# Values in 32 KB rows, one ring of four buffers, and value products moved behind the second half of the scores

## The chip, the cores and the metric

The kernel runs on one core of a Trainium2 chip. The metric is the device time of one execution in microseconds (us); the core has TensorE (PE, its weight loads shown as PEld), VectorE (DVE), ScalarE (ACT), GpSimd (POOL) and SyncE (SP), which work through their own instruction queues in order and wait for one another by semaphores. The loads from HBM are issued by SP, apart from one small one by ACT, and carried by 16 DMA engines.

## The reference

One token (B = S = 1, D = 512) goes through a decode step of grouped-query attention over a cache of 16384 tokens, with 32 query heads of 128 elements, 8 key/value heads and 4 query heads to each of them, and then through a small MLP. All inputs are bf16.

```python
def _A_ref(x, k_cache, v_cache, wq, wo):
    q = (x @ wq).reshape(B, Sq, Hq, Dh).transpose(0, 2, 1, 3)
    k = jnp.repeat(k_cache, rep, axis=1)          # k_cache: 1 x 8 x 16384 x 128
    v = jnp.repeat(v_cache, rep, axis=1)
    scores = jnp.einsum("bhqd,bhkd->bhqk", q, k) * (Dh ** -0.5)
    p = _softmax(scores, axis=-1)
    o = jnp.einsum("bhqk,bhkd->bhqd", p, v)
    return o.transpose(0, 2, 1, 3).reshape(B, Sq, Hq * Dh) @ wo

def _B_ref(x, w1, w2, w3, w4):
    ...
    x1 = x + hs          # hs is 0 for a single token: its shifted parts are all padding
    h2 = _gelu(_layernorm(x1) @ w3) @ w4
    return x1 + h2

h = x + _A_ref(_layernorm(x), ...)
return h + _B_ref(_layernorm(h), ...)
```

The keys and the values of one head are 4 MB each, so the two caches are 64 MB. `wq` and `wo` are 4 MB each, `w3` and `w4` 1.75 MB each.

## The kernel before, in words

**Loading.** `load` (L215) puts every big transfer on SP's queue, in program order. SP holds each issue until the buffer it writes is free, and whatever stands behind it on SP waits too. Keys of a head come as one transfer of 128 rows of 32 KB (`load_k`, L218) into one of two buffers `kb` (`KRING`, L124). Values come as two transfers of 128 rows of 16 KB, one for each half A of the tokens (`load_v`, L230), into three buffers `vb` of half a head (`VRING`, L125); the last head's values go to `kb[0]`. `wq` and later `wo` use the buffer `wqo`, `w3` and `w4` the buffer `kb[1]`. The order on SP is wq, k0, k1, and then in iteration g of the main loop both halves of v(g) and k(g+2), and in iteration 7 the last values and the weights.

**The main loop** (L472) runs over g = 0 to 8. In iteration g it does the scores and the softmax of head g and the value products of head g-1:

- `transpose_keys` (L385): eight DVE block transposes of 1024 words each, tiles t = 0 to 7, from `kb` to `kt`. The one buffer `kt` holds the head being worked on.
- `scores(g, half)` (L395): 16 matmuls of 512 columns for each half of the scores, into the PSUM tile `s_ps`. Four matmuls at a time use the four column groups (`ct`) of the array; the first one on column group ct of a half needs tile t = 4*half + ct, so the last 13 of a half start when its last transpose is done.
- `max_a`, `max_b`, `max_c` (L406, L410, L418): a maximum over all tokens, by a DVE reduction of each half, two small matmuls, a second reduction, and a matmul that spreads it over the partitions; then two ACT exponentials (L425) of 512 columns write the weights `p_sb`. A POOL copy repeats the first columns at its end.
- `weights(g)` (L433): 16 PE transposes of windows of 128 columns, 64 apart, into the two-bank PSUM tile `T_ps` (eight to a bank), and five DVE copies (L441) from it into `pt`.
- `denominator` (L445), and `gather(g-1)` (L462): one DVE copy of `O_ps` to `o_sb` and four fp32 matmuls (each recorded as two) that lay the head's output into `A_ps`.
- `values(g-1, A, qs)` (L450): 16 matmuls of 512 columns for each half A of the tokens. They are placed by hand on PE: the 16 of half 0 between the two halves of the scores, 8 of half 1 before `max_b` and 8 before `max_c`.

In iteration 0, when there are no values yet, three of the next head's key transposes are done early. Iteration 8 has only the values and the gather of head 7.

**The end.** The output is normalised (L520 to L527), multiplied by `wo` (128 matmuls, L533, in four pieces as they land), and goes through the layer norm (`row_sums` L255, `variance` L268, `seeds` L277, `inverse_root` L293), `w3` (L546), Gelu (L558), `w4` (L567) and the store (L573).

`Program.op` (L35) derives the waits: an operation waits for the last writer of what it reads, for the writers and readers of what it writes, and for the last operation of every other engine on a PSUM bank that it touches.

Of the kernel before, what the change touches and what calls it, by code (L numbers as in the profile page):

```python
# [7 lines left out]
BF16 = mybir.dt.bfloat16  # L8
# [102 lines left out]
D = 512  # L111
HQ = 32
# [11 lines left out]
KRING = 2  # L124
VRING = 3  # L125
VT = 64 * DH
KPARTS = 6
# [4 lines left out]
def bass_sequential_preLN__gqa_block_cached__mixer_s_mlp__decode_kernel(  # L132
# [13 lines left out]
    with ExitStack() as ctx:  # L146
# [3 lines left out]

# [33 lines left out]
        p_sb = sb("p_sb", [128, 1024 + 64], BF16)  # L184
        pt = [sb(f"pt{i}", [128, 4, 2, 16, REP], BF16) for i in range(2)]
# [14 lines left out]
        wqo = sb("wqo", [128, NCH * HQ * DH], BF16)  # L200
        kb = [sb(f"kb{i}", [128, 128 * DH], BF16) for i in range(KRING)]
        kt = sb("kt", [128, 128 * DH], BF16)
        vb = [sb(f"vb{i}", [128, VT], BF16) for i in range(VRING)]
        w3_sb = kb[1][:, 0:NCH * FM].rearrange("p (k f) -> p k f", k=NCH)
        w4_sb = kb[1][:, NCH * FM:2 * NCH * FM].rearrange("p (m c) -> p m c", m=NHC)
# [12 lines left out]
        def load_k(g):  # L218
            i = g % KRING
            load(f"k{i}", kb[i][:, :], A_k_cache[0, g].rearrange("(p t) d -> p (t d)", p=128), ("k", i, 0),  # L220
                 also=[("k", i, n) for n in range(1, KPARTS)])

        def value_tile(g, A):

            if g == HKV - 1:
                return kb[0][:, A * VT:(A + 1) * VT], ("k", 0, A)
            i = (2 * g + A) % VRING
            return vb[i][:, :], ("v", i)

        def load_v(g, A):  # L230
            src = A_v_cache[0, g, A * 8192:(A + 1) * 8192, :].rearrange("(p t) d -> p (t d)", p=128)
            dst, key = value_tile(g, A)
            load("v" + "_".join(map(str, key[1:])), dst, src, key)
# [59 lines left out]
        def inverse_root(i, n, by):  # L293

            s, t = st[i], sti[i]
            S, T = ("st", i), ("sti", i)
            v, y = s[:, 4 + n:5 + n], t[:, n:n + 1].bitcast(FP32)
            z = s[:, 8 + n:9 + n]
            vh = s[:, 10 + n:11 + n]
            by(lambda e: e.tensor_scalar(vh, v, -0.5, None, ALU.mult), r=[(S, 4 + n)], w=[(S, 10 + n)])  # L300
            for k in range(3):
                dst, key = (s[:, 6 + n:7 + n], (S, 6 + n)) if k == 2 else (y, (T, n))
                by(lambda e: e.tensor_scalar(z, y, y, vh, ALU.mult, ALU.mult),
                   r=[(T, n), (S, 10 + n)], w=[(S, 8 + n)])
                by(lambda e, dst=dst: e.tensor_scalar(dst, z, 1.5, y, ALU.add, ALU.mult),
                   r=[(S, 8 + n), (T, n)], w=[key])
# [3 lines left out]
        load("wq", wqo[:, :], A_wq.rearrange("(p k) c -> p (k c)", k=NCH), ("wo", 0),  # L310
             also=[("wo", n) for n in range(1, len(WO))])
        load_k(0)
        load_k(1)
# [52 lines left out]
        for h in range(HQ):  # L366
            for k in range(NCH):
                pe(lambda e, h=h, k=k: e.matmul(n_ps[:, h:h + 1],  # L368
                                                wqo[:, k * HQ * DH + h * DH:k * HQ * DH + (h + 1) * DH],
                                                xn[:, k:k + 1], start=(k == 0), stop=(k == NCH - 1)),  # L370
                   r=["xn"] + [("wo", n) for n in range(len(WO))], w=["n"], bank=["mn"])
# [13 lines left out]
        def transpose_keys(g, ts):  # L385
            i = g % KRING
            for t in ts:
                view = lambda x, t=t: x[:, :].bitcast(I32).rearrange("p (x l w) -> p x (l w)", x=2, l=64)[
                    :, :, t * 512:(t + 1) * 512]
                dve(lambda e, i=i, view=view: e.transpose(view(kt), view(kb[i])),  # L390
                    r=[("k", i, n) for n in range(KPARTS)], w=[("kt", t)])

        ktv = kt[:, :].rearrange("p (x l b s e) -> p b e l x s", x=2, l=64, b=2, s=32, e=2)

        def scores(g, half):  # L395
            for n in range(4):
                for ct in range(4):
                    c8 = 4 * half + ct
                    pe(lambda e, g=g, half=half, n=n, ct=ct, c8=c8: e.matmul(  # L399
                        s_ps[32 * ct:32 * ct + 32, half, :],  # L400
                        qb[:, n, g, :, :, :].rearrange("p a u h -> p (a u h)"),
                        ktv[:, n // 2, n % 2, 8 * c8:8 * c8 + 8, :, :],
                        start=(n == 0), stop=(n == 3)),
                       r=["qb", ("kt", c8)], w=[("s", half)], bank=[("s", half)])
# [13 lines left out]
        def max_c(g):  # L418
# [5 lines left out]
            for half in range(2):  # L424
                act(lambda e, half=half, g=g: e.activation(  # L425
                    p_sb[:, half * 512:half * 512 + 512].rearrange("p (l s x) -> p l x s", l=8, x=2),
                    s_ps[:, half, :].rearrange("p (l x s) -> p l x s", l=8, x=2),
                    ACTF.Exp, bias=bias[:, 0:1], scale=float(SCALE), accum_out=acc[g % 2][:, half:half + 1]),
                    r=[("s", half), "bias"], w=[("p", half), ("acc", g % 2)], bank=[("s", half)])
                if half == 0:  # L430
                    P.op("POOL", lambda e: e.tensor_copy(p_sb[:, 1024:1088], p_sb[:, 0:64]), r=[("p", 0)], w=[("p", 2)])  # L431

        def weights(g):  # L433
            for w in range(16):
                pe(lambda e, w=w: e.transpose(T_ps[:, w, :], p_sb[:, w * 64:w * 64 + 128], ident[:, :]),  # L435
                   r=[("p", w // 8), ("p", (w + 1) // 8), "ident"], w=[("T", w // 8)], bank=[("T", w // 8)])
            to = pt[g % 2][:, :, :, :, :].rearrange("p c A l h -> p l (c A) h")
            of = T_ps[:, :, :].rearrange("p w (k o u h) -> p w k o u h", o=2, u=2, h=REP)
            for half, lo, w0, w1, l0 in ((0, 0, 0, 8, 0), (0, 64, 0, 8, 1), (1, 0, 8, 16, 8), (1, 64, 8, 15, 9),
                                         (1, 64, 15, 16, 0)):  # L440
                dve(lambda e, lo=lo, w0=w0, w1=w1, l0=l0: e.tensor_copy(  # L441
                    to[lo:lo + 64, l0:l0 + w1 - w0, :, :], of[lo:lo + 64, w0:w1, :, lo // 64, 0, :]),
                    r=[("T", half)], w=[("pt", g % 2)], bank=[("T", half)])
# [6 lines left out]
        def values(g, A, qs):  # L450
            tile, key = value_tile(g, A)
            for q in qs:
                for ct in range(4):
                    n = 32 * (q // 2) + 8 * ct + 4 * (q % 2)
                    pe(lambda e, q=q, ct=ct, n=n: e.matmul(  # L455
                        O_ps[g % 2][32 * ct:32 * ct + 16, :],
                        pt[g % 2][:, ct, A, 4 * q:4 * q + 4, :].rearrange("p l h -> p (l h)"),
                        tile[:, n * DH:(n + 4) * DH],
                        start=(A == 0 and q == 0), stop=(A == 1 and q == 3)),
                       r=[key, ("pt", g % 2)], w=[("O", g % 2)], bank=[("O", g % 2)])  # L460
# [11 lines left out]
        for g in range(HKV + 1):  # L472
# [6 lines left out]
            if g:  # L479
                values(g - 1, 0, range(4))  # L480
            if g < HKV:
                scores(g, 1)
                max_a(1)
            if g == 0:
                transpose_keys(1, range(0, 1))
            if g:
                values(g - 1, 1, range(2))
            if g < HKV:
                max_b()
            if g:  # L490
                values(g - 1, 1, range(2, 4))
            if g < HKV:
                max_c(g)
            if g == 0:
                transpose_keys(1, range(1, 3))
# [5 lines left out]
            if g < HKV:  # L501
                for A in range(2):
                    load_v(g, A)
                if g + 2 < HKV:
                    load_k(g + 2)
            if g == HKV - 1:
                for n, (lo, hi) in enumerate(WO):
                    load(f"wo{n}", wqo[:, lo * D:hi * D], A_wo.rearrange("(p r) c -> p (r c)", p=128)[:, lo * D:hi * D],
                         ("wo", n))
                w3_in = B_w3.rearrange("(p k) f -> p k f", p=128)  # L510
                for n, (lo, hi) in enumerate(W3):
                    load(f"w3{n}", w3_sb[:, lo:hi, :], w3_in[:, lo:hi, :], ("k", 1, n))
                w4_in = B_w4.rearrange("(p m) c -> p m c", p=128)
                for n, (lo, hi) in enumerate(W4):
                    load(f"w4{n}", w4_sb[:, lo:hi, :], w4_in[:, lo:hi, :], ("k", 1, 2 + n))
# [15 lines left out]
        for r_ in range(32):  # L531
            for q in range(4):
                pe(lambda e, r_=r_, q=q: e.matmul(O_ps[0][32 * q:32 * q + 32, 0:128], copies(o_b[:, r_:r_ + 1], 32),  # L533
                                                  wqo[:, r_ * D + q * 128:r_ * D + (q + 1) * 128],
                                                  start=False, stop=(r_ == 31), skip_group_check=True),
                   r=["o_b", ("wo", piece(WO, r_))], w=[("O", 0)], bank=[("O", 0)])
# [7 lines left out]
        for k in range(NCH):  # L544
            for q in range(4):
                pe(lambda e, k=k, q=q: e.matmul(s_ps[32 * q:32 * q + 32, 0, 0:FQ], hc[:, k, :],  # L546
                                                w3_sb[:, k, q * FQ:(q + 1) * FQ], start=(k == 0), stop=(k == NCH - 1)),
                   r=["hc", ("k", 1, piece(W3, k))], w=[("s", 0)], bank=[("s", 0)])
# [16 lines left out]
        for m in range(NHC):  # L565
            for o in range(4):
# [3 lines left out]
                   r=[("hcol", 2 * m // NHC), ("k", 1, 2 + piece(W4, m))], w=["n"], bank=["mn"])  # L570
# [36 lines left out]
```

## Time and profile before

| | |
|---|---|
| time, median of 3 runs (lowest to highest) | 193.95 us (193.8 to 193.97) |
| time of the profiled execution | 194.09 us |
| its span, first to last instruction | 192.3 us |
| busy: PE / DVE / ACT / POOL | 112.8 / 120.1 / 16.9 / 6.6 us |
| key transposes, L390 (64) | 74.0 us, 1212 ns each |
| score matmuls, L399 (256) | 556 ns each, four at a time |
| value matmuls, L455 (224 and 32) | 529 and 474 ns each, four at a time |
| copies of weights, L441, 64x256 (24) | 286 ns each |
| copies of weights, L441, 64x224 (8) / 64x32 (8) | 278 / 172 ns each |
| exponentials, L425 (16) | 824 ns each |
| mean granted TensorE clock | 0.761 of full speed |

The span is the time in which the core's instructions ran; the rest of the execution's time, 1.8 us, lies around it. Matmul durations contain the way through the array, so a stream of them is read from their starts: four value matmuls follow four others 0.42 us later at half clock and 0.21 us later at full clock. The clock that the throttle grants is 0.5 or 1.0 in this trace and changes every few microseconds. The trace also has a record of each DMA packet: a row of 16 KB is one packet of 613 ns (median of the 16 KB packets), a row of 32 KB one packet of 1214 ns (median of those).

### The profile page before, as it was taken

The numbers are of one execution on the slowest core, as the hardware profiler recorded it, in microseconds if no ns is written. First come the engines' busy times: TensorE is split into PE (matmuls) and PEld (weight loads), VectorE is DVE, ScalarE is ACT, GpSimd is POOL, SyncE is SP. The second block draws the span as 40 slices with busy tenths as digits, with TensorE's granted clock in tenths as the row PEclk, the third lists the DMA queues.
The fourth block names the chain that finished last, engine by engine and source line by source line (L and its number), as shares of the span: only waits on it lengthen the run. The fifth ranks groups of instructions, "written<-read, shape, count | busy, mean of one in ns | idle before, by whom it ended". The sixth has DMA issues, their size and how long they took to land.

```text
span 192.3 us, 2626 instructions
## 1 busy us (share of the span) xinstructions
PE 112.8 (59%) x1106; PEld 55.9 (29%) x1106; DVE 120.1 (62%) x225; ACT 16.9 (9%) x38; POOL 6.6 (3%) x26
## 2 busy tenths in 40 slices
PE   1025045658837766774686558645785676595443
PEld 1025001242234235223422432233223422454311
DVE  4844099499349929964795369546953796303170
ACT  3000000030030030003000300030003000600010
POOL 2000000000000000000000000000000000000060
PEclk9999999999985695588559655975558559669555
DMA  6999999999999999999999999999999999999991
GB/s 232 436 429 429 433 436 426 436 441 433 406 426 464 429 392 426 477 433 392 423 447 419 429 416 433 443 433 416 447 445 412 402 429 423 426 418 421 417 376 48
DMA packets 5066, 79.32 MB, mean 413 GB/s; under 512 B 576, under 2 KB 576, under 8 KB 1344
## 3 DMA queue, kind: packets, MB, share of 16 engines
q1 hardware_dynamic: 5048, 79.17, 96.9%
q8 instruction: 8, 0.13, 0.3%
q14 instruction: 2, 0.02, 0.0%
q10 hardware_dynamic: 8, 0.00, 0.0%
HBM read 79.17 MB, written 0.00 MB: 412 GB/s over the span
## 4 chain that ended last, share of the span: by engine, by line
DMA 40%; DVE 14%; SPq 5%; issue 2%; PE 1%
DMA kb<-in_A_k_cache_dram 30%; DVE kt L390 13%; DMA kb<-in_B_w_dram 10%; SPq L216 5%; DVE mx L407 1%; PE T_ps L435 0%; DVE pt L441 0%; PE mn_ps L567 0%; DVE fin L571 0%; PE A_ps L446 0%; SPq L102 0%; DVE o_sb L464 0%
## 5 line engine op out<-in xcount | busy, mean ns | idle before, releaser
L390 DVE STREAM_TRANSPOSE kt<-kb 128x1024 int32<-128x1024 int32 x64 | 74.0, 1212 | 11.2 <-DMA kb<-in_A_k_cache_dram 11.1
L399 PE MATMUL s_ps<-kt,qb 128*32 128x512 bf16 x256 | 47.5, 556 | 32.3 <-DVE kt L390 32.3
L455 PE MATMUL O_ps<-vb,pt 128*16 128x512 bf16 x224 | 28.9, 529 | 0.0
L399 PEld LDWEIGHTS s_ps<-kt,qb 128*32 128x32 bf16 x256 | 10.6, 113 | 61.9 <-DVE kt L390 54.1
L425 ACT ACTIVATE p_sb<-s_ps,bias 128x512 bf16<-128x512 f32 x16 | 12.8, 824 | 150.1 <-PE mn_ps L419 114.1
L467 PE MATMUL A_ps<-o_sb,zo 128*128 128x128 f32 x64 | 15.7, 422 | 10.3 <-DVE o_sb L464 10.3
L441 DVE COPY pt<-T_ps 64x256 bf16<-64x256 bf16 (+2 forms) x40 | 9.8, 261 | 15.6 <-PE T_ps L435 15.2
L407 DVE TENSOR_REDUCE mx<-s_ps 128x1 f32<-128x512 f32 x16 | 10.8, 677 | 11.9 <-PE s_ps L399 9.9
L435 PE MATMUL T_ps<-ident,p_sb 128*128 128x128 bf16 x128 | 11.8, 250 | 10.9 <-ACT p_sb L425 10.9
L467 PEld LDWEIGHTS A_ps<-o_sb,zo 128*128 128x128 f32 x64 | 13.4, 310 | 11.4 <-DVE o_sb L464 11.4
L435 PEld LDWEIGHTS T_ps<-ident,p_sb 128*128 128x128 bf16 x128 | 8.9, 112 | 12.9 <-ACT p_sb L425 12.7
L455 PEld LDWEIGHTS O_ps<-vb,pt 128*16 128x16 bf16 x224 | 9.4, 114 | 9.8 <-issue 8.5
L368 PE MATMUL mn_ps<-xn,wqo 128*128 128x1 bf16 x128 | 3.6, 165 | 9.1 <-DMA wqo<-in_A_wq_dram 9.1
L412 PE MATMUL mn_ps<-ident_f,mx 128*1 128x128 f32 x32 | 7.3, 323 | 2.5 <-DVE mx L407 2.5
L464 DVE COPY o_sb<-O_ps 128x512 f32<-128x512 f32 x8 | 5.5, 691 | 4.9 <-PE O_ps L455 4.6
L431 POOL COPY p_sb<-p_sb 128x64 bf16<-128x64 bf16 x8 | 1.9, 236 | 160.7 <-ACT p_sb L425 160.7
L368 PEld LDWEIGHTS mn_ps<-xn,wqo 128*128 128x128 bf16 x128 | 3.5, 104 | 9.2 <-issue 9.2
L415 DVE TENSOR_REDUCE nm<-mn_ps 1x4 f32<-1x256 f32 x8 | 3.2, 406 | 3.7 <-PE mn_ps L412 3.7
L533 PE MATMUL O_ps<-wqo,o_b 128*32 128x128 bf16 x128 | 3.0, 253 | 3.0 <-DMA wqo<-in_A_wo_dram 1.7
L412 PEld LDWEIGHTS mn_ps<-ident_f,mx 128*1 128x1 f32 x32 | 2.3, 90 | 7.7 <-DVE mx L407 5.4
L419 PEld LDWEIGHTS mn_ps<-nm,nscale 1*128 1x128 f32 x16 | 2.5, 198 | 5.5 <-DVE nm L415 5.5
L258 DVE TENSOR_SCALAR_CACHE_REDUCE hr<-O_ps 128x128 f32<-128x128 f32 x2 | 0.6, 292 | 5.5 <-PE O_ps L533 4.8
(79 smaller groups left out, 55.9 us busy)
## 6 DMA issues: line engine op xcount, KB each, us to landing
kb<-in_A_k_cache_dram SPq DMA_DIRECT2D x8, 4096.0 KB, 26.7
vb<-in_A_v_cache_dram SPq DMA_DIRECT2D x14, 2048.0 KB, 24.4
wqo<-in_A_wq_dram SPq DMA_DIRECT2D x1, 4096.0 KB, 12.4
kb<-in_A_v_cache_dram SPq DMA_DIRECT2D x2, 2048.0 KB, 26.6
wqo<-in_A_wo_dram SPq DMA_DIRECT2D x2, 1280.0 KB, 32.8
kb<-in_B_w_dram SPq DMA_DIRECT2D x1, 1344.0 KB, 22.9
wqo<-in_A_wo_dram SPq DMA_DIRECT2D x1, 1024.0 KB, 36.2
kb<-in_B_w_dram SPq DMA_DIRECT2D x1, 640.0 KB, 24.8
```

Of the source, the lines that this page charges most:

```text
L216: P.op(by, lambda e: e.dma_start(dst, src), w=[key, *also], dma=name)
L368: pe(lambda e, h=h, k=k: e.matmul(n_ps[:, h:h + 1], wqo[:, k * HQ * DH + h * DH:k * HQ * DH + (h + 1) * DH], xn[:, k:k + 1], start=(k == 0 ...
L390: dve(lambda e, i=i, view=view: e.transpose(view(kt), view(kb[i])), r=[("k", i, n) for n in range(KPARTS)], w=[("kt", t)])
L399: pe(lambda e, g=g, half=half, n=n, ct=ct, c8=c8: e.matmul(s_ps[32 * ct:32 * ct + 32, half, :], qb[:, n, g, :, :, :].rearrange("p a u h -> ...
L407: dve(lambda e: e.tensor_reduce(mx[:, half:half + 1], s_ps[:, half, :], AX.X, ALU.max), r=[("s", half)], w=[("mx", half)], bank=[("s", half)])
L412: pe(lambda e, half=half: e.matmul(m_ps[0:1, half * 128:half * 128 + 128], mx[:, half:half + 1], ident_f[:, :], start=True, stop=True), r= ...
L425: act(lambda e, half=half, g=g: e.activation(p_sb[:, half * 512:half * 512 + 512].rearrange("p (l s x) -> p l x s", l=8, x=2), s_ps[:, hal ...
L435: pe(lambda e, w=w: e.transpose(T_ps[:, w, :], p_sb[:, w * 64:w * 64 + 128], ident[:, :]), r=[("p", w // 8), ("p", (w + 1) // 8), "ident"] ...
L441: dve(lambda e, lo=lo, w0=w0, w1=w1, l0=l0: e.tensor_copy(to[lo:lo + 64, l0:l0 + w1 - w0, :, :], of[lo:lo + 64, w0:w1, :, lo // 64, 0, :]) ...
L455: pe(lambda e, q=q, ct=ct, n=n: e.matmul(O_ps[g % 2][32 * ct:32 * ct + 16, :], pt[g % 2][:, ct, A, 4 * q:4 * q + 4, :].rearrange("p l h -> ...
L464: dve(lambda e, g=g: e.tensor_copy(o_sb[g % 2][:, :], O_ps[g % 2][:, :]), r=[("O", g % 2)], w=[("osb", g % 2)], bank=[("O", g % 2)])
L467: pe(lambda e, g=g, j=j: e.matmul(A_ps[:, 0:128], zo[:, j, 112 - 16 * g:240 - 16 * g], o_sb[g % 2][:, j * 128:(j + 1) * 128], start=False, ...
```

## The change

All five big buffers and the value ring are replaced by four buffers `rb` of 32 KB a partition. One list, `ORDER`, gives the sequence of the loads: wq, k0, k1, then v0, k2, v1, k3, and so on to v7, wo, and the MLP weights; the n-th one uses buffer n mod 4. A head's values are one transfer of 128 rows of 32 KB, laid out like the keys.

With that, a partition's tokens lie otherwise in the score tile: the columns of a half are ordered (x, l, s) where they were permuted to (l, s, x) by the exponential's output. The exponential now writes plainly. The windows of the PE transposes stand 32 columns apart, and there are 32 of them in four fills of eight (f = 0 to 3); fills 0 and 2 use bank 0 of `T_ps` and are copied by DVE, fills 1 and 3 use bank 1 and are copied by ACT. A copy takes 32 partitions with 128 elements each. In fill 3 three of the four copies are split where the tokens wrap, so that it has seven. That makes 8 DVE copies and 11 ACT copies for each head. The POOL copy is of 96 columns.

All value products stand behind both halves of the scores: 8 before `max_b`, 8 before `max_c`, 16 after `max_c` and ahead of the PE transposes. In `inverse_root` the DVE form of one operation becomes `scalar_tensor_tensor`.

```diff
-KRING = 2
-VRING = 3
-VT = 64 * DH
-KPARTS = 6
+RING = 4
+ORDER = [("wq", 0), ("k", 0), ("k", 1)]
+ORDER += [x for g in range(HKV) for x in (("v", g), ("k", g + 2)) if x[1] < HKV] + [("wo", 0), ("ffn", 0)]
+SLOT = {x: n % RING for n, x in enumerate(ORDER)}
+QB, PB, FB = SLOT["wq", 0], SLOT["wo", 0], SLOT["ffn", 0]
+RPARTS = 6
...
-        p_sb = sb("p_sb", [128, 1024 + 64], BF16)
-        pt = [sb(f"pt{i}", [128, 4, 2, 16, REP], BF16) for i in range(2)]
+        p_sb = sb("p_sb", [128, 1024 + 96], BF16)
+        pt = [sb(f"pt{i}", [128, 4, 32, REP], BF16) for i in range(2)]
...
-        wqo = sb("wqo", [128, NCH * HQ * DH], BF16)
-        kb = [sb(f"kb{i}", [128, 128 * DH], BF16) for i in range(KRING)]
+        rb = [sb(f"rb{i}", [128, 128 * DH], BF16) for i in range(RING)]
         kt = sb("kt", [128, 128 * DH], BF16)
-        vb = [sb(f"vb{i}", [128, VT], BF16) for i in range(VRING)]
...
+        def load_whole(i, src):
+            load(f"r{i}", rb[i][:, :], src, ("r", i, 0), also=[("r", i, n) for n in range(1, RPARTS)])
+
+        def load_tokens(kind, g):
+            src = A_k_cache if kind == "k" else A_v_cache
+            load_whole(SLOT[kind, g], src[0, g].rearrange("(p t) d -> p (t d)", p=128))
...
-        ktv = kt[:, :].rearrange("p (x l b s e) -> p b e l x s", x=2, l=64, b=2, s=32, e=2)
+        ktv = kt[:, :].rearrange("p (x l b s e) -> p b e x l s", x=2, l=64, b=2, s=32, e=2)
...
-                        ktv[:, n // 2, n % 2, 8 * c8:8 * c8 + 8, :, :],
+                        ktv[:, n // 2, n % 2, :, 8 * c8:8 * c8 + 8, :],
...
-                    p_sb[:, half * 512:half * 512 + 512].rearrange("p (l s x) -> p l x s", l=8, x=2),
-                    s_ps[:, half, :].rearrange("p (l x s) -> p l x s", l=8, x=2),
+                    p_sb[:, half * 512:half * 512 + 512], s_ps[:, half, :],
...
-            for w in range(16):
-                pe(lambda e, w=w: e.transpose(T_ps[:, w, :], p_sb[:, w * 64:w * 64 + 128], ident[:, :]),
-                   r=[("p", w // 8), ("p", (w + 1) // 8), "ident"], w=[("T", w // 8)], bank=[("T", w // 8)])
...
+            of = T_ps[:, :, :].rearrange("p w (c a u h) -> p c w a u h", c=4, a=4, u=2)
+            for f in range(4):
+                b = f % 2
+                for w in range(8 * f, 8 * f + 8):
+                    pe(lambda e, w=w: e.transpose(T_ps[:, w % 16, :], p_sb[:, w * 32:w * 32 + 128], ident[:, :]),
+                       r=[("p", w // 16), ("p", (w + 3) // 16), "ident"], w=[("T", b)], bank=[("T", b)])
+                for a in range(4):
+                    n = 8 * f + a
+                    for lo, hi in ((n, min(n + 8, 32)), (32, n + 8)):
+                        if lo >= hi:
+                            continue
+                        args = (pt[g % 2][32 * a:32 * a + 32, :, lo % 32:lo % 32 + hi - lo, :],
+                                of[32 * a:32 * a + 32, :, 8 * b + lo - n:8 * b + hi - n, a, 0, :])
+                        if b == 0:
+                            dve(lambda e, args=args: e.tensor_copy(*args),
+                                r=[("T", b)], w=[("pt", g % 2, 0)], bank=[("T", b)])
+                        else:
+                            act(lambda e, args=args: e.copy(*args),
+                                r=[("T", b)], w=[("pt", g % 2, 1)], bank=[("T", b)])
...
-            if g:
-                values(g - 1, 0, range(4))
-            if g < HKV:
                 scores(g, 1)
                 max_a(1)
...
             if g:
-                values(g - 1, 1, range(2))
+                values(g - 1, range(2))
             if g < HKV:
                 max_b()
             if g:
-                values(g - 1, 1, range(2, 4))
+                values(g - 1, range(2, 4))
             if g < HKV:
                 max_c(g)
+            if g:
+                values(g - 1, range(4, 8))
...
             if g < HKV:
-                for A in range(2):
-                    load_v(g, A)
+                load_tokens("v", g)
                 if g + 2 < HKV:
-                    load_k(g + 2)
+                    load_tokens("k", g + 2)
```

## The prediction

> **What bounds the kernel now.** I read the page first, then the chain of waits, then the timeline of iterations 1, 3 and 5, then the granted clock by stretches.
>
> ```profile
> span 192.3 us, 2626 instructions
> ...
> DMA  6999999999999999999999999999999999999991
> ...
> q1 hardware_dynamic: 5048, 79.17, 96.9%
> ```
>
> The DMA engines never pause between the first load and the last, so bytes set the end. The chain of waits agrees, its long pieces being transfers. But compute is close behind:
>
> ```profile
> 57.34 1.23 DVE L390 STREAM_TRANSPOSE kt<-kb 128x1024 int32<-128x1024 int32 x1
> ...
> 74.40 6.87 DVE L390 STREAM_TRANSPOSE kt<-kb 128x1024 int32<-128x1024 int32 x6
> ...
> 84.18 1.10 PE L399 MATMUL s_ps<-kt,qb 128*32 128x512 bf16 x13 [0.66 <-DVE kt L390]
> ...
> 87.62 0.82 ACT L425 ACTIVATE p_sb<-s_ps,bias 128x512 bf16<-128x512 f32 x1 [15.47 <-PE mn_ps L419]
> ...
> 112.11 6.88 DVE L390 STREAM_TRANSPOSE kt<-kb 128x1024 int32<-128x1024 int32 x6 [2.03 <-DMA kb<-in_A_k_cache_dram]
> ```
>
> Iteration 2 begins at 57.34 and iteration 3 at 74.40 with no wait for a key: a compute period of 17.06 us. Iterations 5, 6 and 7 begin at 112.11, 131.62 and 151.13, as keys land, every 19.51 us. Compute starts late (k0 is the second load, and iteration 0 is longer), catches up 2.45 us an iteration, and waits for keys only from iteration 4. So the loop may grow by about 2.4 us before it can never catch up, and by less before its lag outlives iteration 7.
>
> The third thing is the clock:
>
> ```profile
> core 0: us, PE busy (x) PEld busy (x) DVE busy (x) ACT busy (x) POOL busy (x), PEclk, DMA share, GB/s
> ...
> 79.80:83.20 3.40, 3.03 (x28) 0.82 (x20) 3.40 (x5) 0.00 (x0) 0.00 (x0) 0.50 1.11 477
> 83.20:90.10 6.90, 4.39 (x54) 2.38 (x53) 2.69 (x7) 1.65 (x4) 0.24 (x1) 0.99 0.96 413
> ...
> 134.40:137.90 3.50, 2.47 (x18) 0.67 (x21) 3.50 (x4) 0.00 (x0) 0.00 (x0) 0.50 1.00 426
> 137.90:141.30 3.40, 2.60 (x20) 0.55 (x12) 3.40 (x4) 0.00 (x0) 0.00 (x0) 0.50 1.10 472
> 141.30:144.70 3.40, 3.30 (x32) 1.24 (x33) 0.74 (x3) 0.00 (x0) 0.00 (x0) 0.50 0.98 417
> ```
>
> The clock goes to full after a stretch of 3.4 us with 3.03 us of PE work (2.88 before the rise at 158.3), and stays half after 2.60. In iteration 3 that burst is the first half's scores and the 16 value products right behind them (79.08 to 82.67). In iteration 6 the burst fell across two stretches, and the period was 18.1 us (131.62 to the end of L464 at 149.7) instead of 17.1.
>
> **The change, part by part.**
>
> *Rows of 32 KB.* 2048 packets of 613 ns become 1024 of 1214 ns: (1255.4 - 1243.1) / 16 = 0.77 us less for the DMA engines, which is the whole gain if they stay the bound: a floor of 191.5 us span. The ring: k(g+2) waits on SP for the transposes of g as before, v(g+1) for the products of g-1 alone; k2 and v1 go out earlier. Keys take 26.7 us from issue to landing, of which 4 MB at 427 GB/s is 9.8, so 17 us of queue lie ahead of an issue; a lag of 5 to 9 us doesn't empty it: 0.
>
> *Two of four fills on DVE* (L441). Counted from the first exponential E (87.62): the PE transposes start at E+0.93 and the five copies end at E+3.26 (89.59 + 1.29). After: fill 0 needs only the first exponential; its eight transposes are 0.06 apart at full clock, so the last starts at E+1.35, and copies begin 0.27 after such a start (89.32 to 89.59), E+1.62. A copy of 128 elements lies between the 64x32 row (172 ns) and the 64x256 row (286), I take 225; four make 0.90, E+2.52. Then fill 2 waits for this bank: transposes to E+2.99, copies E+3.26 to E+4.16. **+0.90 us** on the DVE queue, behind which stand L464 and the next head's transposes. The bounds of the copies move it by 0.45 either way. At half clock transposes are 0.107 apart (+0.35 for each fill) and the 16 value products behind `max_c` take 1.7 us in PE's idle 1.2 us (E-0.29 to E+0.93), +0.5: together +2.1. At full clock they take 0.86 and fit.
>
> *Value products moved.* Their 1.7 us no longer stand between the halves of the scores. That saves nothing, since the second half waits for its last transpose (84.12). But it takes away the second half of the burst. By my count of starts a stretch there now holds 2.4 to 2.9 us, on the threshold, for about 1.1 us of the 3.4 us in which a stretch may begin. I take one iteration in four as warmed there; the others warm only in the dense work after the last transpose, 2.4 to 5.8 us behind it. The price is shown by iteration 1, at half clock:
>
> ```profile
> 48.93 1.89 PE L399 MATMUL s_ps<-kt,qb 128*32 128x512 bf16 x13 [0.52 <-DVE kt L390]
> ...
> 53.45 0.82 ACT L425 ACTIVATE p_sb<-s_ps,bias 128x512 bf16<-128x512 f32 x1 [13.01 <-PE mn_ps L419]
> ```
>
> 4.52 us from these scores to the exponential against 3.44 in iteration 3: +1.08, three times in four, **+0.8**. Fills at half clock in a quarter of the iterations add 0.25 x 1.2 = **+0.3**.
>
> The Trainium skill ("TensorE: Matmul & The Clock Gate", Part 1, "What's actually happening") says that full speed comes after at least one busy window of about 3.4 us, sustained, the windows running freely. The trace has rises after 2.88 of 3.4 us, so less than a full window does; read strictly, the page makes the second rival below.
>
> *ACT copies.* 11 of 0.20 (the 1x1 row of L516) to 0.49 us (128x224, L558). They end at E+5.5 to E+7.5 and are read 10 us into the next iteration: 0, except in iteration 7. *Nothing:* plain exponential output (its 824 ns fall in with 128x224 in 486, so no stride price is seen; at most -0.1); the scores' column order (strided L399 556 ns, plain L455 529); POOL's 96 columns (0.24 us, needed 2 us later); the new DVE form in `inverse_root` (L272 takes 0.21 like L305).
>
> **The sum.** Period 17.06 + 0.9 + 0.8 + 0.3 = 19.1 us. Iteration 0: its DVE copies begin at 40.95 behind transposes, and two serial fills of 0.90 with a refill at half clock of 1.1 end at 43.95, not 42.35: +1.6. Iteration 1 was cold already: +1.1. Iteration 2 begins at 57.34 + 2.7 = 60.0, iteration 7 at 60.0 + 5 x 19.1 = 155.5, where its keys landed at 150.5.
>
> From there: to `o_b` (L527) 25.44 (151.13 to 176.57) + 0.8 + 0.5 (gather and value products behind the later copies; 0 to 1.2); the 128 products with `wo`, which now lies ready, 0.05 + 2.96 (1.30 + 1.04 + 0.62); to the first product with `w4` 5.8 (181.28 to 187.09); 56 of these 2.3; to the end 2.4 (189.94 to 192.3). 40.3 us, so the span is 195.8, +3.5. The profiled execution took 194.09, 0.14 above the median; on 193.95 I forecast **197.5 us**, and 194.5 to 201.5 for this case.
>
> **Rivals.**
> *DMA stays the bound* (0.17): PE stays warm, by a burst that suffices or by the dense work lasting into the next head. Then the period is 17.06 + 0.9 = 18.0, compute catches up 1.5 us an iteration, and the floor rules: 193.95 - 0.8 = 193.2. It decides from a period under 18.4: (192.3 - 40.3 - 60.0) / 5. For it: the threshold lies between 2.60 and 2.88 us, where the new burst lies too. Against: iteration 6 missed with 2.60.
> *Clock always late* (0.10): only a whole stretch of work counts, so every iteration pays 1.08 and most fills are cold (+1.8): period 19.9, iteration 7 at 60.3 + 99.5, span 200.1, 201.8 us. Against: 2.88 of 3.4 did.
> *ACT changes tables between exponential and copy* (0.03): no row shows a copy between exponentials; L516's load took 1.28 us, and one ahead of each exponential makes the period 20.4, 204 us. The Trainium skill ("ScalarE: Activation LUTs", "Table sets: the hidden batching unit") has copy in every set, which speaks against it.
> *Both limits meet* (0.05): a period near 18.4 gives no change, about 194.
>
> **How the numbers follow.** The forecast has 0.65. The rivals on top have 0.13, so the range ends at 201.5; to leave out no more than 2 in 10 it must take in the floor, so it begins at 193.1. A difference of 0.2% is what a measurement of this kernel can tell. Faster 0.17, same 0.05, slower 0.78.
>
> **What would show it.** After: fewer DMA packets by 1024, and no idle stretch before about 189; iterations 3 to 7 begin with no wait for keys, 18.5 to 20 us apart; clock half between the last key transpose and `max_b` in most iterations; L441 copies of about 225 ns with a wait of 0.7 us between the fills; L533 waits for `o_b` and no longer for `wo`. The prediction is wrong if iterations 4 to 7 still wait for keys, if the stretch from last transpose to exponential stays at 3.5 us, or if copies of 128 elements cost as little as 172 ns.

## The result and the profile after

The changed kernel takes 195.55 us (median of 6 runs, 194.8 to 196.24) against 193.96 us (6 runs): a ratio of 1.0078, 95% interval 1.0066 to 1.0091. It is slower, as forecast, by 1.6 us and not by 3.5. Its profiled execution took 194.80 us, the shortest of the six, with a span of 193.0 us.

From the page of the changed kernel:

```profile
span 193.0 us, 2990 instructions
...
DMA  6999999999999999999999999999999999999980
...
q1 hardware_dynamic: 3896, 79.17, 96.3%
q8 instruction: 9, 0.15, 0.3%
...
DVE 52%; PE 27%; DMA 12%; issue 6%; ACT 2%; SPq 0%; ACTq 0%
```

The DMA engines still never pause before the tail, with 1152 packets fewer (1024 of the rows, 128 of 4 bytes). But the chain that ended last now lies on DVE and PE (the last line above: shares of the span by engine), where it was led by transfers before:

```profile
DMA 40%; DVE 14%; SPq 5%; issue 2%; PE 1%
```

In this execution, the shortest, the loads end almost with the compute: the last data packet ends at 189.69, and the last eight products with `w4` start at 190.18, when their weights have just landed (190.14), 0.19 us behind the group ahead of them, where the other groups follow at 0.10. From the last data packet to the end of the span are 3.3 us here, as in the kernel before; in a second trace, of a run of 195.88 us (h4 below), they are 4.4, and there compute alone is last. The row of q8 becomes important below.

The timeline (start, duration, engine, line, and the idle time before with what ended it):

```profile
59.90 1.24 DVE L381 STREAM_TRANSPOSE kt<-rb 128x1024 int32<-128x1024 int32 x1
...
79.38 1.23 DVE L381 STREAM_TRANSPOSE kt<-rb 128x1024 int32<-128x1024 int32 x1
...
89.15 1.89 PE L390 MATMUL s_ps<-kt,qb 128*32 128x512 bf16 x13 [0.52 <-DVE kt L381]
...
93.44 0.69 ACT L416 ACTIVATE p_sb<-s_ps,bias 128x512 bf16<-128x512 f32 x1 [13.82 <-PE mn_ps L410]
...
94.93 0.92 DVE L439 COPY pt<-T_ps 32x128 bf16<-32x128 bf16 x4 [1.57 <-PE T_ps L429]
...
155.37 3.48 DVE L381 STREAM_TRANSPOSE kt<-rb 128x1024 int32<-128x1024 int32 x3
```

Iterations 2 and 3 begin at 59.90 and 79.38, and iteration 7 at 155.37, none with a wait for keys. The 13 score matmuls behind the last transpose take 1.89 us, as in iteration 1 of the kernel before, where iterations 2 to 5 had 1.06 to 1.10. From there to the exponential are 4.29 us (3.44 before), and 4.91 in iteration 2.

The clock by stretches of iteration 3:

```profile
core 0: us, PE busy (x) PEld busy (x) DVE busy (x) ACT busy (x) POOL busy (x), PEclk, DMA share, GB/s
81.80:85.20 3.40, 2.37 (x14) 0.67 (x16) 3.40 (x4) 0.00 (x0) 0.00 (x0) 0.50 0.99 424
85.20:88.60 3.40, 1.92 (x8) 0.28 (x3) 3.40 (x4) 0.00 (x0) 0.00 (x0) 0.50 0.92 395
88.60:92.00 3.40, 2.88 (x29) 0.97 (x32) 1.19 (x2) 0.00 (x0) 0.00 (x0) 0.50 1.01 434
92.00:95.40 3.40, 3.11 (x44) 1.67 (x36) 1.02 (x6) 1.47 (x5) 0.27 (x1) 1.00 1.08 458
```

The two stretches around the first half's scores hold 2.37 and 1.92 us of PE work; the clock rises only after 2.88 us of work in the stretch behind the last transpose, at 92.0, between the maximum and the exponential. In the kernel before it rose at 83.2. In all eight iterations of the changed kernel the first reduction of the second half follows the last transpose by 1.98 us, as at half clock before (1.15 to 1.20 at full clock).

### The profile page after: what moved, and what is told of

It reads as the page before. It is cut to its first block, busy times and chain, and to the rows that moved or that the text cites. A ratio compares the mean times of both kernels' runs of the same rounds, so it can differ in the third digit from the quotient of the medians.

```text
span 193.0 us, 2990 instructions
## 1 busy us (share of the span) xinstructions
PE 119.5 (62%) x1234; PEld 58.3 (30%) x1234; DVE 123.7 (64%) x249; ACT 33.1 (17%) x126; POOL 6.9 (4%) x26
## 2 busy tenths in 40 slices
DMA packets 3916, 79.34 MB, mean 411 GB/s; under 512 B 448, under 2 KB 448, under 8 KB 1216
## 4 chain that ended last, share of the span: by engine, by line
DVE 52%; PE 27%; DMA 12%; issue 6%; ACT 2%; SPq 0%; ACTq 0%
DVE kt L381 37%; DMA rb<-in_A_k_cache_dram 12%; PE s_ps L390 8%; PE O_ps L456 7%; DVE pt L439 7%; PE T_ps L429 5%; DVE mx L398 3%; ACT p_sb L416 2%; PE mn_ps L403 2%; PE mn_ps L410 2%; PE A_ps L467 1%; PE O_ps L531 1%; PE mn_ps L565 1%; DVE o_sb L464 1%; DVE nm L406 1%
## 5 line engine op out<-in xcount | busy, mean ns | idle before, releaser
L381 DVE STREAM_TRANSPOSE kt<-rb 128x1024 int32<-128x1024 int32 x64 | 74.0, 1210 | 4.8 <-DMA rb<-in_A_k_cache_dram 4.8
L456 PE MATMUL O_ps<-rb,pt 128*16 128x512 bf16 x256 | 28.5, 484 | 0.0
L439 DVE COPY pt<-T_ps 32x128 bf16<-32x128 bf16 x64 | 14.1, 220 | 18.1 <-PE T_ps L429 17.4
L429 PE MATMUL T_ps<-ident,p_sb 128*128 128x128 bf16 x256 | 19.7, 232 | 6.2 <-DVE pt L439 4.3
L442 ACT COPY pt<-T_ps 32x128 bf16<-32x128 bf16 (+6 forms) x88 | 17.7, 226 | 11.7 <-PE T_ps L429 11.1
L429 PEld LDWEIGHTS T_ps<-ident,p_sb 128*128 128x128 bf16 x256 | 15.8, 104 | 12.1 <-DVE pt L439 5.8
L467 PE MATMUL A_ps<-o_sb,zo 128*128 128x128 f32 x64 | 10.6, 316 | 7.7 <-DVE o_sb L464 7.7
L467 PEld LDWEIGHTS A_ps<-o_sb,zo 128*128 128x128 f32 x64 | 8.9, 215 | 8.8 <-DVE o_sb L464 8.8
L456 PEld LDWEIGHTS O_ps<-rb,pt 128*16 128x16 bf16 x256 | 8.3, 101 | 6.1 <-issue 3.3
L359 PE MATMUL mn_ps<-xn,rb 128*128 128x1 bf16 x128 | 3.6, 165 | 9.2 <-DMA rb<-in_A_wq_dram 9.2
## 6 DMA issues: line engine op xcount, KB each, us to landing
rb<-in_B_w_dram SPq DMA_DIRECT2D x1, 1344.0 KB, 18.3
```

What stands on the lines that cost most here:

```text
L359: pe(lambda e, h=h, k=k: e.matmul(n_ps[:, h:h + 1], wq_sb[:, k * HQ * DH + h * DH:k * HQ * DH + (h + 1) * DH], xn[:, k:k + 1], start=(k == ...
L381: dve(lambda e, i=i, view=view: e.transpose(view(kt), view(rb[i])), r=[("r", i, n) for n in range(RPARTS)], w=[("kt", t)])
L429: pe(lambda e, w=w: e.transpose(T_ps[:, w % 16, :], p_sb[:, w * 32:w * 32 + 128], ident[:, :]), r=[("p", w // 16), ("p", (w + 3) // 16), " ...
L439: dve(lambda e, args=args: e.tensor_copy(*args), r=[("T", b)], w=[("pt", g % 2, 0)], bank=[("T", b)])
L442: act(lambda e, args=args: e.copy(*args), r=[("T", b)], w=[("pt", g % 2, 1)], bank=[("T", b)])
L456: pe(lambda e, q=q, ct=ct, t=t: e.matmul(O_ps[g % 2][32 * ct:32 * ct + 16, :], pt[g % 2][:, ct, 4 * q:4 * q + 4, :].rearrange("p l h -> p ...
```

## The experiments

Each was run beside the kernel before on one chip (194.06 us for the e runs, 193.98 for the g runs, 194.04 for the h runs). "Last data packet" is the end of the last packet of the loads in the trace of the run.

**e1: the kernel before with the value products moved, and nothing else.**

```diff
-            if g:
-                values(g - 1, 0, range(4))
...
-                values(g - 1, 1, range(2))
+                values(g - 1, 0, range(2))
...
-                values(g - 1, 1, range(2, 4))
+                values(g - 1, 0, range(2, 4))
...
                 max_c(g)
+            if g:
+                values(g - 1, 1, range(4))
```

> The kernel before with nothing changed but the place of the value products: 8 before max_b, 8 before max_c, 16 behind max_c. Clock theory: in every iteration from 2 on the first reduction of the second half starts 1.98 us after the last key transpose (1.15 to 1.20 before, in all but one) and the exponential about 4.7 us after it (3.5 before), so the compute period is 17.06 + 1.2 = 18.3 us; that still catches up with keys that come every 19.5, so the time stays within 0.3% of before: 193.9 to 194.5. Rival, that the moved products themselves are the cost and not the clock: they stand in an idle stretch of PE, the exponential follows the last transpose by 3.5 us, and the period stays at 17.1. A period of 19 or more here would mean that the move alone makes the whole loss.

Measured: 194.35 us, ratio 1.0018 (1.0007 to 1.0029). The reduction follows the last transpose by 1.98 us in seven iterations and by 1.56 in iteration 4, the exponential by 4.4 to 5.0 us from iteration 2 on. Periods without a wait are 18.0, 18.6 and 18.1 us, and iterations 6 and 7 begin with their keys. So the move costs about 1.2 us an iteration (the mean of these periods is 18.2, against 17.06), and alone it is nearly hidden. The last data packet ends 0.3 us later than in the trace of before (189.26 against 188.97); why was not found.

**e2: the changed kernel with fills 0 and 1 copied by DVE, 2 and 3 by ACT.**

```diff
-                        if b == 0:
+                        if f < 2:
```

> The changed kernel with DVE copying fills 0 and 1 and ACT copying fills 2 and 3, so that DVE no longer waits 0.7 us for the refill of its bank. If the serial fills are 0.8 us of the period: copies end 3.4 us after the exponential, not 4.05, the period is 19.1 - 0.65 = 18.45, iteration 7 begins at about 150.6 with a wait for its keys, and the time is that of the DMA engines, 193.2 to 193.8. If only the clock counts and the copies are covered by something else: no change, 195.5.

**e3: 16 products without use between the halves of the scores.**

```diff
+        def idle_products(g):
+            for q in range(4):
+                for ct in range(4):
+                    pe(lambda e, q=q, ct=ct, g=g: e.matmul(
+                        O_ps[(g - 1) % 2][32 * ct:32 * ct + 16, :],
+                        qb[:, q, g, 0:2, :, :].rearrange("p a u h -> p (a u h)"),
+                        ktv[:, q // 2, q % 2, :, 8 * ct:8 * ct + 8, :], start=True, stop=True),
...
+                if g:
+                    idle_products(g)
                 scores(g, 1)
```

> The changed kernel with 16 added matmuls of 512 columns between the halves of the scores, on keys that are there, into a PSUM tile that the value products then overwrite; they keep PE busy where the value products stood before and compute nothing that is used. Clock theory: the clock rises before the second half's scores, reduction 1.2 us and exponential 3.5 us behind the last transpose, period 17.9 us, iteration 7 at about 150.6 with its keys, and the DMA engines set the time: 193.2 to 193.8. Rival, that the lost time is work on the DVE and PE queues: more PE work cannot help, 195.5 or more.

**e4: half of the value products put back between the halves.**

```diff
+            if g:
+                values(g - 1, range(4))
             if g < HKV:
                 scores(g, 1)
...
-                values(g - 1, range(2))
+                values(g - 1, range(4, 6))
...
-                values(g - 1, range(2, 4))
+                values(g - 1, range(6, 8))
...
-                values(g - 1, range(4, 8))
```

> The changed kernel with 16 of its 32 value products put back between the halves of the scores. A head's values now land whole, 9.8 us behind its successor's keys, so PE waits there when compute has no lag. Clock theory: the lag settles at some 3 us, where the values are there in time, the clock rises as in the kernel before, and the time is 193.2 to 193.8. Rival, that the wait for whole values eats the gain: the second half's scores start late, the period is 19.5 with a lag of 5 us or more, 195 or more.

The three gave 194.8, 194.76 and 194.76 us (ratios 1.0041, 1.0041 and 1.0039, intervals from 1.0027 to 1.0053). Each did in the loop what it was to do. In e2 the copies end 3.37 us behind the exponential for 4.05, and iteration 7 begins at 151.04 with a wait for keys. In e3 the exponential follows the last transpose by 3.5 us in four of the seven iterations from 1 to 7 (4.5 in iterations 2 and 5, where the clock was up but fell just behind the last transpose, at 68.90 and 123.52, after stretches with 1.2 us of PE work; 4.7 in iteration 7, where it rose only at 164.48), and iteration 7 begins at 150.86 with a wait for keys. In e4 periods alternate between 18.3 and 19.4 us, and iteration 7 begins at 153.78 without a wait; what ends its chain is a load all the same. Two lines of the timeline of e3 show the warm case:

```profile
87.36 1.06 PE L390 MATMUL s_ps<-kt,qb 128*32 128x512 bf16 x13 [0.73 <-DVE kt L381]
...
90.76 0.69 ACT L416 ACTIVATE p_sb<-s_ps,bias 128x512 bf16<-128x512 f32 x1 [12.94 <-PE mn_ps L410]
```

So the loop's extra time is both the clock and the serial fills, and taking away either is enough for the loads to end the kernel. But I had expected 193.2 to 193.8, and none came near it. The chain of waits of e2 ends in a transfer:

```profile
169.71 20.65 DMA rb<-in_B_w_dram
```

and the last data packet ends at 189.91, 189.95 and 189.66 in the three, where the kernel before has 188.97. The stream itself is longer, though its packets sum to less (186.7 us an engine, 187.15 before). That stood against my floor, and a second theory was needed.

**What the packet records show.** The records name no engine, but a packet starts 4 ns before the end of the one ahead of it, so the 16 engines can be followed; each carries 8 rows of every transfer. One engine of the changed kernel around 49.6 us:

```
start us   end us   bytes  queue
  48.426   49.642   32768  q1
  49.638   50.707   16384  q8 (instructions)
  50.693   52.405   32768  q1      1712 ns, the others take 1216
```

A fetch of 16 KB of code runs on one of the engines that carry the data, and costs it 1069 + 496 = 1.57 us. In the changed kernel, the engines with no fetch end their streams at 186.5 to 186.8, those with one at 187.9 to 188.3 (two others took 8 KB fetches, and end at 187.1 and 188.6), and the one with two, as I follow it the first and the ninth (18.4 and 185.9), at 189.70. That is 3.1 us, the price of two fetches, behind the engines with none. PE's fetches come about every 256 of its recorded instructions. Before has 2221 of them and 8 fetches; the changed kernel has 2485 and 9. The last stretches of the stream:

```profile
188.40:188.80 0.40, 0.00 (x0) 0.00 (x0) 0.40 (x2) 0.14 (x1) 0.30 (x2) 0.50 0.10 36
188.90:189.10 0.20, 0.20 (x12) 0.20 (x16) 0.20 (x1) 0.00 (x0) 0.20 (x1) 0.50 0.03 10
189.20:189.60 0.40, 0.40 (x28) 0.40 (x20) 0.06 (x1) 0.00 (x0) 0.32 (x2) 0.50 0.05 20
```

(the changed kernel; columns as above, the DMA share next to last). A share of 0.03 to 0.05 is no more than one engine of 16 (0.06), still at work when the others are done.

**g1: the kernel before with more code.**

```diff
-        for h in range(HQ):
+        for twice, h in [(t, h) for t in range(2) for h in range(HQ)]:
             for k in range(NCH):
                 pe(lambda e, h=h, k=k: e.matmul(n_ps[:, h:h + 1],
```

> The kernel before with the 128 small products of wq done twice, in a stretch in which PE waits for the first keys: 256 more PE instructions (2221 to 2477 recorded) and no other work. In the trace of before PE's code comes in 8 fetches of 16 KB, one about every 256 instructions, each on another DMA engine; an engine with a fetch ends its stream at about 188.4, one without at 186.7. In the changed kernel (2485 instructions) there are 9, the ninth on the engine that had the first, which ends at 189.7. Code theory: a ninth fetch near 182 us, one engine's stream ends at 189.7 to 190.3, and the time is 194.6 to 195.2. Rival, that the later end of the stream belongs to the 32 KB rows or to the ring: 8 or 9 fetches alike, 194.0.

Measured: 195.15 us, ratio 1.0059 (1.0047 to 1.0072). From its page:

```profile
q8 instruction: 9, 0.15, 0.3%
```

The ninth fetch comes at 181.3, and the last data packet ends at 190.02, 1.05 us later than in before. 256 instructions that run while PE has nothing else to do cost 1.2 us at the other end of the kernel.

**g2: e2 with less code.**

```diff
-            for k in range(NCH):
+            for k in range(1):
...
-                                                xn[:, k:k + 1], start=(k == 0), stop=(k == NCH - 1)),
+                                                xn[:, k:k + 1], start=True, stop=True),
```

> The kernel of e2 (fills 0 and 1 on DVE) with only the first of the four terms of each product with wq, so that q is a quarter of its sum: 192 PE instructions fewer (2293), none of them in a stretch that anything waits for. Code theory: 8 fetches, no engine with two of them, the last packet ends at 188.3 to 188.6 and not at 189.9, 193.1 to 193.5: the floor that the 32 KB rows should give. Rival, rows or ring: 194.8 as in e2.

Measured: 193.78 us, ratio 0.9985 (0.9977 to 0.9994), 1.0 us under e2, and 0.3 over my range; last data packet at 188.75.

**g3: e2 with fewer PE instructions for the same results.** The products of wq become 32 matmuls of one row by 512 columns in the four column groups, and eight PE transposes turn the row.

```diff
-        o_sb = [sb(f"o_sb{i}", [128, 512], FP32) for i in range(2)]
+        o_sb = [sb(f"o_sb{i}", [128, 512], BF16) for i in range(2)]
...
-        zo = sb("zo", [128, 4, 240], FP32)
+        zo = sb("zo", [128, 4, 240], BF16)
...
+        for c in range(2):
+            for k in range(NCH):
+                for j in range(4):
+                    pe(lambda e, c=c, k=k, j=j: e.matmul(
+                        s_ps[32 * j:32 * j + 1, c, :], xn[:, k:k + 1],
+                        wq_sb[:, k * HQ * DH + (2 * j + c) * 512:k * HQ * DH + (2 * j + c) * 512 + 512],
+                        start=(k == 0), stop=(k == NCH - 1)),
...
```

> A whole kernel with fewer PE instructions (about 2245): that of e2, with the products of wq as 32 matmuls of 512 columns and 8 PE transposes in the place of 128 small matmuls, and o_sb and zo in bf16, so that each gather has 4 matmuls in the place of 8 passes. Code theory: 8 fetches, last packet at 188.3 to 188.6, 193.1 to 193.5, faster than both kernels. Rival, rows or ring: 194.8.

Measured: 193.33 us, ratio 0.9967 (0.9955 to 0.9979), faster than both kernels; last data packet at 188.21, span 191.5 us. My count of fetches was off in g2 and g3: there are nine, but the first comes only at 42 us and the ninth at 188.6 and 189.0, when the data have all but landed. What counts is that no engine takes two within the stream. Because no fetch meets the first keys, they are there 1.3 us earlier (iteration 0 begins at 22.66, 23.95 in the changed kernel).

**g4: the kernel before with a longer period.**

```diff
+            if 0 < g < 7:
+                for _ in range(4):
+                    dve(lambda e, g=g: e.tensor_copy(junk[:, :], O_ps[(g - 1) % 2][:, :]),
+                        r=[("O", (g - 1) % 2), "junk"], w=["junk"], bank=[("O", (g - 1) % 2)])
```

> The kernel before with four DVE copies of 0.7 us into a scratch tile at the end of iterations 1 to 6, and nothing else: a compute period of about 20 us, so that iteration 7 begins at about 160 without a wait for keys and its tail meets wo and the weights already landed. If a tail that waits for no DMA runs at full clock, as the changed kernel's does: 37 us from the start of iteration 7 to the end, 128 products of wo in 2.0 us, span about 197, 198.8 us. If the tail keeps the half clock of the rows that I took from before: 39 us, 3.0 us for the 128 products, span 199, 200.9 us.

Measured: 202.35 us, ratio 1.0432 (1.0413 to 1.0451). Iteration 7 began at 161.58, later than I said, and the end came 39.5 us after it (span 201.0). The first theory fell; the second gave the tail within half a microsecond (39), and its 200.9 missed because the periods were longer than 20. The tail of g4:

```profile
180.78 3.59 PE L455 MATMUL O_ps<-kb,pt 128*16 128x512 bf16 x32
...
187.79 3.57 PE L538 MATMUL O_ps<-wqo,o_b 128*32 128x128 bf16 x128 [1.29 <-DVE o_b L532]
```

and that of the changed kernel:

```profile
176.13 1.90 PE L456 MATMUL O_ps<-rb,pt 128*16 128x512 bf16 x32
...
181.44 1.97 PE L531 MATMUL O_ps<-rb,o_b 128*32 128x128 bf16 x128 [1.29 <-DVE o_b L525]
```

Neither waits for a load. In g4 the clock rises 9.1 us into iteration 7 and falls again at 16.0, before the tail; in the changed kernel the late burst lets it rise at 15.1, and it stays up until 187.6. The same products take half the time. By stretches (columns as above, the granted clock third from the end):

```profile
175.00:183.40 8.40, 6.27 (x177) 4.53 (x177) 1.91 (x6) 1.63 (x4) 0.00 (x0) 1.00 1.00 411
178.00:191.40 13.40, 10.49 (x177) 7.15 (x177) 2.60 (x7) 0.00 (x0) 0.00 (x0) 0.63 0.73 294
176.00:184.60 8.60, 6.44 (x170) 3.78 (x169) 1.92 (x7) 0.16 (x1) 0.00 (x0) 0.85 1.01 412
```

These are the changed kernel, g4, and the changed kernel's second trace (h4). That the late burst is the reason is argued and rests on one trace of the old order. The phase counts too: in h3, which has the new order, the clock was half just during the products with `wo`, and they took 3.53 us as in g4.

**h1: g3 with the values in rows of 16 KB.** `load_tokens` issues two transfers for a head's values, of half a row each.

> The kernel of g3 with each head's values loaded by two transfers of 128 rows of 16 KB, into the same buffer and the same places. Row theory (2048 packets of 613 ns against 1024 of 1214): the last data packet ends 0.8 us later than in g3 (188.2), 194.0 to 194.2. Rival, that the row size counts for nothing and g3 owes all to its smaller code: 193.3.

Measured: 194.31 us, ratio 1.0013 (1.0004 to 1.0021); last data packet at 188.97, 0.76 us later than in g3, against 0.77 by the packets' sums. The time lies 0.1 us over my range. The rows are worth what their packets say.

**h2: the kernel before with the smaller code of g3.**

> The kernel before with the smaller PE code of g3 (products of wq as 32 wide matmuls and 8 transposes; o_sb and zo in bf16): about 1980 PE instructions for 2221, one fetch fewer. Code theory: before has no engine that takes two fetches within its stream, so one fewer spares nothing at the end: 193.6 to 194.0. Rival, that less code helps by itself: 193.3 as in g3.

Measured: 194.52 us, ratio 1.0027 (1.0016 to 1.0038); last data packet at 189.30. Less code doesn't help by itself, which was the question; but the time lies 0.5 us over my range, and this I can't explain: with rows of 16 KB the engines couldn't be followed without ambiguity.

**h3: the changed kernel with that smaller code**, its copies as they are.

> The changed kernel with that smaller PE code and its own copies. No fetch falls on the DMA engines before 42 us, so the first keys come 1.3 us earlier, and none falls twice on one engine within the stream; the compute period stays 19.1 us. If compute ends the changed kernel: iteration 7 begins at about 154.3 without waiting for its keys, 194.0 to 194.5, slower than g3. If the late DMA engine alone ends it: 193.3 as g3. If code counts for nothing: 195.5.

Measured: 194.23 us (193.39 to 195.76), ratio 1.0012 (0.9992 to 1.0031), 0.9 us above g3. Iteration 7 begins at 154.28 without a wait. The traced execution is one of the faster (193.68), and it ends with the loads, 3.3 us behind the last data packet (188.44). So no trace shows a slow execution of h3: that compute's lag, which varies from run to run, is what is left over g3 is argued from the spread, which g3 does not have (193.16 to 193.64).

**h4: the changed kernel once more.**

> The changed kernel once more, for a second trace: its six times spread from 194.8 to 196.24, and the trace is of the fastest. If the spread is the phase of the clock against the iterations: another mean of the period (19.1 in the first trace), no E-X under 4.2, nine fetches again, and the end 37 to 38.5 us behind the start of iteration 7.

One time, 195.88 us, span 194.09. Iterations begin at 60.14, 78.88, 98.26, 116.94, 136.11 and 155.63, a mean period of 19.1 again, where I had expected another; nine fetches; the end 38.5 us after the start of iteration 7, 0.8 us more than in the first trace, most of it in the value products and the gather of the last head (26.9 us to `o_b` for 26.0), in which the clock was partly low. So the spread shown here is not in the period but in the tail (0.8 us) and in the start of iteration 7 (0.3).

## Why the prediction was right and where it was wrong

- **The loop: right.** Forecast: iteration 2 at 60.0, a period of 19.1, iteration 7 at 155.5. Measured: 59.90, 19.09 (155.37 less 59.90, by 5), 155.37. The parts were less exact. Two serial fills cost 0.80 us (copies end 4.05 us behind the exponential, 3.25 before), not 0.9. The clock cost 1.2 us (4.67 on average from last transpose to exponential in iterations 2 to 6, 3.48 before in iterations 2 to 5) and not 0.8, since none of the iterations warmed early, where I had given one in four. Fills at half clock cost at most 0.15, where I had 0.3: the clock had risen by then. So the period came out right partly by luck, by errors of -0.1, +0.4 and about -0.3 that cancel. Iteration 0 too: its terms add up to 43.85 and not to the 43.95 I wrote, and 43.93 was measured. (The keys of iteration 7 landed at 151.1 before, not at 150.5; nothing hangs on it.) e1, e2 and e3 show the first two causes singly.
- **The tail: the step that failed.** "40.3 us, so the span is 195.8" measured 37.6 (193.0 less 155.37), and 38.5 in the second trace, which lies nearer the median. Its terms, forecast and measured in the two traces: to `o_b` 26.75, and 26.0 and 26.9; the products with `wo` 3.0, and 2.0 twice; to the first product with `w4` 5.8, and 5.4 and 5.5; these products 2.3, and 1.8 and 1.7; the end 2.4 each time. I had taken the durations from the tail of before and not asked what the clock and the loads had done to them there. Of the 128 products with `wo`, 48 ran there at half clock, in two pieces that waited for the load; now all 128 run at full clock. The products with `w4` run at half clock in both kernels (four in 0.10 us), but before they waited for their weights in pieces. Part of the 5.4 is the new DVE form in `inverse_root`: 0.16 us for 0.21, three times, where I had nothing. The change that costs the loop its clock left it up in the tail in both traces; g4, with the old order, had a tail of 39.5 us. That the moved burst is the reason, and not the phase of the clock, is not settled.
- **The floor: wrong by 1.5 us, and mostly hidden by the lag.** I gave 191.5 us of span if the DMA engines set the end, and put the fetching of code at nothing. The gain of 0.77 us from larger rows is real (h1), but e2, e3 and e4 reach only 193.0 to 193.2, since 128 more PE transposes bring a ninth code fetch (g1, g2, g3). The two fastest executions of the changed kernel, with 193.0, lie at that floor. My first rival, at 193.2, could not have come about in this kernel.
- **The whole**, by medians: of the changed kernel's 195.55 us, about 0.8 go with the lag alone (e2 to e4), and a further 1.5 with the code (e2 to g3); g3 is then 0.65 under before. By executions: two of the six (194.80 and 194.81) are as fast as e2 to e4, which the loads end, and the other four (195.2 to 196.2) are later, as the second trace shows, by compute. The loss forecast was 3.5 us; nearly all of the 1.9 us between forecast and median lie in the tail. The prediction gives its range two lower ends, 194.5 and 193.1; the median lies above both.
- The rival of a table change on ACT is out: ACT's copies take 226 ns on average and run between the exponentials with no load there. The exponentials fell from 824 to 683 ns with plain output, more than the 0.1 us I had allowed; nothing waits for that in the loop but 0.14 us of the first fill.

## What to carry to other kernels

Where a hand-placed order keeps TensorE's clock up, moving work moves the clock too: price the new order with durations at the clock it will have, in the loop and in the tail, and ask of each duration taken from an old trace whether it waited for a load there. When DMA engines set the end, it is the last engine that does, and code is a transfer like any other: count the instruction fetches, and see whether one engine takes two. Before a floor is trusted, look at when each engine of the old trace ends, not only at their mean share.

## What was not expected of the hardware

- A 16 KB fetch of PE code takes a data engine for 1069 ns and slows the packet beside it from 1216 to 1712 ns. One comes for about every 256 recorded PE instructions, and the ninth within the stream fell on an engine that had one already.
- Code placed early acts late: 256 instructions run before the first keys moved the end of the kernel by 1.2 us (g1).
- The share of PE work in a stretch does not tell alone whether the clock rises. It rose after 2.88 us of 3.4 in the kernel before and did not after 2.60. In the changed kernel it rose after 2.87 and 2.89 (from 126.1 and 88.6), but not after 2.90 (136.4 to 139.8), of which 2.08 were the gather's fp32 matmuls; in e4 it did not after 3.00 (55.4 to 58.8). What else counts is not known.
